# GpSimd's step additions on 64-bit words, and the products O x 1/sum on VectorE, in a fused gated mix of softmax and linear attention

## The chip, the cores and the metric

One core of a Trainium2 chip runs the whole program. The metric is the device time of one execution in microseconds (us), the median of several runs. The profile is one further execution, recorded by the hardware profiler. It tells of TensorE (PE, with its weight loads as PEld), VectorE (DVE), ScalarE (ACT), GpSimd (POOL) and the queue of SyncE (SP), which issues most DMAs.

## The reference

Two attention blocks read the same x (2048 rows, 512 columns, bf16) and are mixed row by row with a gate g. H is 32 heads of 16 columns.

```
x = A_x
g = sigmoid((x * gate_w).sum(-1, keepdims=True))
# A: softmax attention
q, k, v = heads of x @ A_wqkv
p = softmax(q k^T * Dh**-0.5)
a = (p v, heads joined) @ A_wo
# B: linear attention
phi(t) = where(t > 0, t + 1, exp(t)) + 1e-6
num = phi(q) (phi(k)^T v);  den = phi(q) sum(phi(k)) + 1e-6
b = (num / den, heads joined) @ B_wo
return g * a + (1 - g) * b
```

## The kernel before, in words

The work is one long sequence of score tiles. A *unit* is one tile of scores for one head: 128 keys by 512 queries. Heads go in groups of eight (t8, four groups), queries in four blocks of 512 (qc), and each group and block makes two rounds of four heads each (half), 32 rounds in all. A round has 64 units, the whole kernel 2048. PE multiplies three or four units side by side (f_mm, line 685, Qpad and KT into PSUM). Each unit's exponential is then made in one of two ways:

- ScalarE makes it exactly: one ACTIVATE (line 2071) takes two or three PSUM banks, 1024 or 1536 columns, and writes bf16 tiles PT. PE multiplies each with V once.
- VectorE takes a unit as a *claim*: one TENSOR_SCALAR (line 1565) evicts the scores to int16 in DP, so that the bits, read as f16, are a piecewise linear 2^x. One such pattern is not exact enough, so each claimed unit is used as three patterns (STEPS, line 31: the pattern itself and the pattern plus 342 and plus 683), each multiplied with V in its own scaling (WEIGHTS, line 30; the scaled copies of V are written at line 925). Four claimed units share one buffer of DP, of which there are 13 (line 236), and the two patterns with a constant added each fill a further buffer.

These additions, the *step additions*, take 128 x 2048 int16 values. Function try_close (line 1587) makes them. Either VectorE adds the constant to int16 (line 1606), or GpSimd does (line 1609): there a pair of int16 patterns is read as one int32 word, and a two-operand addition adds a word of the small tile `steps` that holds the constant twice. `steps` is written by two GpSimd memsets at the start (line 735).

At the end of a pair of rounds the accumulated numerator and the sum of the softmax lie in `oraw` (evicted by VectorE, line 1306). Small DMAs collect the sums, VectorE inverts them (line 1279), a DMA broadcasts 1/sum to `rbc`, and the product oraw x rbc goes to `OT` (line 1294). With OT_POOL = 1 the product is GpSimd's except in the last eight rounds, where it is VectorE's.

The order of all instructions is laid down when the program is built, by a planner that keeps a clock for each engine. It books each instruction with a duration (for instance POOL_ADD, line 447, for a step addition on GpSimd) and gives the next piece of work to whoever is free by its clocks: pool_go (line 494) hands an addition to GpSimd if it can start there soon, pump (line 571) gives VectorE what is left, can_claim (line 1521) decides whether VectorE takes another unit from ScalarE, depending among other things on free DP buffers. So a booked duration changes the order on every engine. An engine runs its instructions in the order laid down; where one needs another engine's result it waits on a semaphore. GpSimd's instructions also wait for the last VectorE instruction that had SBUF operands alone (line 530, _emit).

The start: the first rows of x and the first slices of the weights are loaded; GpSimd writes some constants (lines 702 to 764), among them a 128 x 128 identity `identb` (a memset, line 736, and an affine select, line 737) and the masks `maskK` and `maskQ`; PE transposes x with the identity (line 692), VectorE and ScalarE copy the transposes to xT (lines 1909 and 1907), PE multiplies xT with the weights, VectorE evicts the first queries with `maskQ` (line 887), and the first units follow. Between the memset and the affine select the program carries one instruction that names a library of GpSimd code, number 0. The profile has no row for such an instruction.

The last round has its own end: what has been accumulated is copied out once, the remaining products with V are accumulated in another layout (128x52 matmuls of Vaug with DP and PT), then normalised, transposed and multiplied with the output weights.

Of the kernel before, what the change touches and what calls it, by code (L numbers as in the profile page):

```python
# [9 lines left out]
ALU = mybir.AluOpType  # L10
# [2 lines left out]
BF16 = mybir.dt.bfloat16  # L13
I32 = mybir.dt.int32
I16 = mybir.dt.int16
U16 = mybir.dt.uint16

STATS = {}
# [11 lines left out]
WEIGHTS = (1.0, 203 / 256, 161 / 256)  # L30
STEPS = (0, 342, 683)
NG4 = len(STEPS)
Y_EXP = 12


# [177 lines left out]
def bass_gated_mix__mha_block__linear_attn_block__prompt_kernel(  # L213
# [33 lines left out]
    with ExitStack() as es:  # L247
        _cnt = [0]

        def SB(shape, dt, name):  # L250
            _cnt[0] += 1
            return es.enter_context(nc.sbuf_tensor(f"{name}_{_cnt[0]}", list(shape), dt))
# [27 lines left out]
        V20 = NG * VG  # L280
        Z0 = V20 + 2 * (NG4 - 1) * (V2C + PAD)
        Vraw = SB([128, Z0 + 32], BF16, "Vaug")
# [5 lines left out]
        def v_scaled(par, z, kb, n=1):  # L288

            c = V20 + ((NG4 - 1) * par + z - 1) * (V2C + PAD) + (kb - KB2) * 8 * VC  # L290
            return Vraw[:, c:c + n * 8 * VC]
# [11 lines left out]
        DP = SB([128, NB, NTU], BF16, "DP")  # L303
# [5 lines left out]
        rbc = SB([128, 512], FP32, "rbc")  # L309
        dev = SB([128, 2, 128], FP32, "dev")  # L310
        flag = SB([128, 1], I32, "flag")
        steps = SB([128, 4], I16, "step")
        epool = SB([128, 2, 512], BF16, "epool")
        KVbd = SB([128, NCC, 128], BF16, "KVbd")
        Zsel = SB([128, NCC, 8], BF16, "Zsel")
# [38 lines left out]
        PO = _Eng("pool", SEM("s_pool"))  # L354
# [19 lines left out]
        R = _Res  # L374
# [20 lines left out]
        r_OT = [[R(f"OT{t}_{q}") for q in range(NQC)] for t in range(NT8)]  # L395
        r_rraw = [R(f"rraw{k}") for k in range(8)]
        r_dev, r_flag = R("dev"), R("flag")
        r_step = R("step")
        r_e = [R("e0"), R("e1")]
        r_phiK = [[R(f"phiK{s}_{k}") for k in range(4)] for s in range(2)]  # L400
        r_phi2 = [R(f"phi2{k}") for k in range(NTB // 2)]
# [42 lines left out]
        YIELD_SOON = 0.5  # L444
        POOL_TT = 1.3
        POOL_V = 0.9
        POOL_ADD = 1.97
        OT_POOL = 1
        V2_POOL = 0

        def conflicts(op_, reads, writes):
# [96 lines left out]
        def op(E, fn, reads=(), writes=(), dur=0.2, issue=None):  # L548
            settle(reads, writes)
            return _emit(E, fn, reads, writes, dur, issue)  # L550
# [140 lines left out]
        def f_tr(o, i):  # L691
# [12 lines left out]
           dur=1.6)  # L704
# [9 lines left out]
        for t in range(1, NQC):  # L714
            for cc in range(NCD):
                dma(xT[:, cc, 512 * t:512 * (t + 1)], x2[512 * t:512 * (t + 1), 128 * cc:128 * (cc + 1)], semXT[cc][t],
                    writes=[r_xT[cc][t]], total_after=16, transpose=True, E=SP, lands=5.5)
# [13 lines left out]
                                                   pattern=pattern, channel_multiplier=mult), reads=[w], writes=[w])  # L731

        op(PO, lambda: nc.gpsimd.memset(warm[:], 0.0), writes=[r_warm])
        for z in range(1, NG4):
            op(PO, lambda z=z: nc.gpsimd.memset(steps[:, 2 * z - 2:2 * z], STEPS[z]), writes=[r_step], dur=0.1)  # L735
        op(PO, lambda: nc.gpsimd.memset(identb[:], 0.0), writes=[r_ident])
        op(PO, lambda: nc.gpsimd.affine_select(out=identb[:], in_=identb[:], compare_op=ALU.not_equal,
                                               fill=1.0, base=0, pattern=[[-1, 128]], channel_multiplier=1),
# [813 lines left out]
        def claim(r, u, b, beside, in_group=False):  # L1552
# [7 lines left out]
            if not in_group:  # L1560
# [3 lines left out]
                r_bank[b].tw = max(r_bank[b].tw, PE.t + 0.08)  # L1564
            push(0 if in_group else 1, [(lambda: nc.vector.tensor_scalar(DP[:, i, 512 * k:512 * (k + 1)].bitcast(I16),  # L1565
                                                                     bank_ap(b), FRAC - Y_BIAS4, Y_BIAS4, op0=ALU.max, op1=ALU.add),
# [5 lines left out]
        def add_products(i, z, k, r, u):  # L1572
            pv_pending.append((r, u, [(DP[:, i, 512 * k:512 * (k + 1)].bitcast(F16), z)], r_DP[i][k], Fraction(1, NG4)))

# [12 lines left out]
        def try_close():  # L1587

            while closing:
                i, us, zs = closing[0]  # L1590
                z = len(zs) + 1
                if z == NG4:
                    closing.popleft()
                    continue
                free = free_buffers()
                early = us[0][0] > acc_round[0]
                if len(free) < (LAZY if early else 1):
                    return False
                if not zs and sum(1 for it in items if it.prio == 3) >= (EARLY_ADDS if early else MOST_ADDS):
                    return False  # L1600
                i2 = free[0]
                zs.append(i2)
                n = 512 * len(us)
                y = DP[:, i, 0:n].bitcast(I16)
                mine_, out_ = r_DP[i][0:len(us)], r_DP[i2][0:len(us)]
                ops = (lambda z=z, i2=i2, y=y, n=n: nc.vector.tensor_single_scalar(DP[:, i2, 0:n].bitcast(I16), y, STEPS[z], ALU.add),  # L1606
                       mine_, out_, d_sb(n, 0.25), None)
                if n == NTU:
                    ops = (ops[0], mine_ + [r_step], out_, ops[3], None, POOL_ADD, lambda z=z, i2=i2, y=DP[:, i, 0:n].bitcast(I32), n=n: nc.gpsimd.tensor_tensor(  # L1609
                        DP[:, i2, 0:n].bitcast(I32), y, steps[:, 2 * z - 2:2 * z].bitcast(I32).to_broadcast([128, n // 2]), ALU.add))  # L1610
                push(3, [ops])
                of_round[iseq[0]] = us[0][0]
                for k, (r, u) in enumerate(us):
                    add_products(i2, z, k, r, u)
            return True
# [319 lines left out]
        for c in range(2):  # L1935
            for st, w, b, pcs in pair:
                fns, _, dur, mac, mode = pcs[c]
# [50 lines left out]
        while True:  # L1988
# [72 lines left out]
            for c, eb in extras:  # L2061
# [4 lines left out]
                     dur=QK_T, mac=0.053 * len(fns), mode="rows")  # L2066
            for c, eb in extras:
                claim(c[0], c[1], eb, True, in_group=True)
            STATS["claims %d+%d" % (len(us), len(extras))] = STATS.get("claims %d+%d" % (len(us), len(extras)), 0) + 1
            n = 512 * len(us)  # L2070
# [3 lines left out]
               dur=d_act(n), issue=0.055 + n * 8.34e-4)  # L2074
# [59 lines left out]
        while pv_pending:  # L2134
            if not pv_step(PE.t, force=True):
# [9 lines left out]
                 writes=[r_bank[tbank]], dur=0.3)  # L2145
# [8 lines left out]
           writes=[r_bad], dur=0.25)  # L2154
# [15 lines left out]
        for k in range(NPRE):  # L2170
# [6 lines left out]
            if k == 0:  # L2177
# [4 lines left out]
                         writes=[r_bank[tbank]], dur=0.1)  # L2182
# [47 lines left out]
        for t8 in range(NT8):  # L2230
# [11 lines left out]
            for qc in range(NQC):  # L2242
                for h in range(8):
# [4 lines left out]
                                                                      None, op0=ALU.mult),  # L2248
                       reads=[r_Q2, r_mask], writes=[r_Q[0]])
                    for k in range(4):  # L2250
# [4 lines left out]
                           writes=[r_sm] + r_rdB)  # L2255
# [16 lines left out]
        for tb in range(NTB):  # L2272
            s3 = tb % NOUTT
            pe_macro(out_fns(bank_ap(tb % 4), tb, order_out), reads=[r_OT[t][tb // 4] for t in range(NT8)] + [r_OBT[tb], r_woA, r_woB],
                     writes=[r_bank[tb % 4]])
# [87 lines left out]
```

## Time and profile before

| | us |
|---|---|
| median of 3 runs | 675.92 (675.24 to 676.07) |
| span of the profiled execution, first to last instruction | 673.6 |
| ScalarE busy | 660.1 (98%) |
| TensorE busy | 654.8 (97%) |
| VectorE busy | 575.6 (85%) |
| GpSimd busy | 550.6 (82%) |

The profiled execution has no time of its own beside its span; the median is 2.3 us above the span. The granted TensorE clock is 0.999 of full speed.

In rows of groups, the columns are: line of the kernel, engine, operation, output<-inputs with shapes and types, count | busy time in us, mean duration in ns | idle time of the engine just before these instructions and what ended most of it. A row of the waits says who waited for whom, the total in us, how often, and the longest. A row of the timeline or of the chain begins with the start in us and the length in us. A row for one line gives the shortest, median and longest duration in ns, and the first and last start. A DMA row gives the tiles, the count, KB each and the median time from issue to landing in us. ScalarE's instructions overlap, so that the mean duration is longer than the distance between two starts.

### The profile page before, as it was taken

The numbers are of one execution on the slowest core, as the hardware profiler recorded it, in microseconds if no ns is written. First come the engines' busy times: TensorE is split into PE (matmuls) and PEld (weight loads), VectorE is DVE, ScalarE is ACT, GpSimd is POOL, SyncE is SP. The second block draws the span as 40 slices with busy tenths as digits, with TensorE's granted clock in tenths as the row PEclk, the third lists the DMA queues.
The fourth block names the chain that finished last, engine by engine and source line by source line (L and its number), as shares of the span: only waits on it lengthen the run. The fifth ranks groups of instructions, "written<-read, shape, count | busy, mean of one in ns | idle before, by whom it ended". The sixth has DMA issues, their size and how long they took to land.

```text
span 673.6 us, 19206 instructions
## 1 busy us (share of the span) xinstructions
PE 654.8 (97%) x8078; PEld 199.8 (30%) x8078; DVE 575.6 (85%) x968; ACT 660.1 (98%) x715; POOL 550.6 (82%) x311
## 2 busy tenths in 40 slices
PE   8999999999999999999999999999999999999997
PEld 4322223333223332333222323323323222222223
DVE  4589889889887886888988998999889998989894
ACT  6999999999999999999999999999999999999995
POOL 5098889887889997788986989778788888898883
PEclk9999999999999999999999999999999999999999
DMA  9900101001010021101001010010211401010011
GB/s 212 261 3 12 24 2 33 3 11 27 1 35 2 18 50 36 32 2 30 6 10 36 9 40 12 16 29 13 47 25 25 51 25 42 10 41 27 20 40 44
DMA packets 44816, 22.96 MB, mean 34 GB/s; under 512 B 33976, under 2 KB 40568, under 8 KB 44728
## 3 DMA queue, kind: packets, MB, share of 16 engines
q1 hardware_dynamic: 42712, 20.12, 13.8%
q10 hardware_dynamic: 2016, 1.57, 0.9%
q8 instruction: 66, 1.08, 0.7%
q14 instruction: 22, 0.18, 0.1%
HBM read 8.00 MB, written 2.10 MB: 15 GB/s over the span
## 4 chain that ended last, share of the span: by engine, by line
ACT 89%; PE 7%; DVE 2%; DMA 1%; POOL 0%; issue 0%; SPq 0%; DVEq 0%; ACTq 0%
ACT PT L2071 87%; PE ps L685 7%; ACT epool L970 2%; DVE DP L1565 1%; DMA outt<-in_A_wqkv_dram 1%; POOL DP L1609 0%; DMA rsum<-oraw 0%; DVE DP L2173 0%; DVE KT L859 0%; DVE Qpad L887 0%; DVE OB L1098 0%; DVE oraw L1306 0%; SPq L608 0%; DVE rraw L1279 0%; PE ps L692 0%
## 5 line engine op out<-in xcount | busy, mean ns | idle before, releaser
L2071 ACT ACTIVATE PT<-ps 128x1024 bf16<-128x1024 f32 (+1 forms) x675 | 648.2, 1156 | 1.0 <-PE ps L685 0.7
L1609 POOL TENSOR_TENSOR DP<-DP,step 128x1024 int32<-128x1024 int32 x278 | 526.8, 1924 | 99.9 <-DVE DP L1565 27.6
L1565 DVE TENSOR_SCALAR DP<-ps 128x512 int16<-128x512 f32 x654 | 432.5, 684 | 69.5 <-PE ps L685 63.2
L685 PE MATMUL ps<-Qpad,KT 32*128 32x512 bf16 x2048 | 264.6, 384 | 10.4 <-ACT PT L2071 4.5
L685 PE MATMUL ps<-DP,Vaug 128*32 128x512 f16 x1949 | 206.8, 384 | 1.5 <-DVE oraw L1306 0.7
L685 PE MATMUL ps<-PT,Vaug 128*32 128x512 bf16 x1384 | 174.3, 384 | 0.6 <-DVE Vaug L914 0.5
L685 PEld LDWEIGHTS ps<-Qpad,KT 32*128 32x128 bf16 x2048 | 66.6, 91 | 270.3 <-ACT PT L2071 242.7
L685 PEld LDWEIGHTS ps<-DP,Vaug 128*32 128x32 bf16 x1949 | 49.7, 94 | 66.1 <-issue 41.3
L685 PEld LDWEIGHTS ps<-PT,Vaug 128*32 128x32 bf16 x1384 | 42.1, 95 | 46.7 <-issue 36.7
L685 PE MATMUL ps<-warm 128*32 128x512 bf16 (+1 forms) x270 | 45.8, 386 | 1.1 <-POOL step L735 1.1
L1606 DVE TENSOR_SCALAR DP<-DP 128x2048 int16<-128x2048 int16 (+1 forms) x50 | 33.1, 689 | 0.0
L685 PE MATMUL ps<-xT,wA 128*32 128x512 bf16 x432 | 32.6, 384 | 0.0
L1294 POOL TENSOR_TENSOR OT<-oraw,rbc 128x512 bf16<-128x512 f32 x12 | 15.6, 1299 | 10.9 <-DVE DP L1606 7.2
L970 ACT ACTIVATE epool<-ps 128x512 bf16<-128x512 f32 x32 | 23.4, 732 | 0.0
L1306 DVE COPY oraw<-ps 128x512 f32<-128x512 f32 x31 | 21.1, 681 | 0.7 <-PE ps L685 0.5
L685 PE MATMUL ps<-xT,wB 128*32 128x512 bf16 x256 | 19.7, 384 | 0.0
L685 PE MATMUL ps<-wB,xT 128*32 128x512 bf16 x256 | 19.3, 384 | 0.0
L685 PE MATMUL ps<-woA,OT 128*32 128x512 bf16 (+1 forms) x226 | 19.1, 384 | 0.0
L975 DVE SCALAR_TENSOR_TENSOR phi<-ps,epool 128x512 bf16<-128x512 f32 x24 | 16.3, 679 | 0.0
L685 PEld LDWEIGHTS ps<-warm 128*32 128x32 bf16 (+1 forms) x270 | 11.4, 98 | 13.6 <-issue 11.8
L859 DVE CAST KT<-ps 128x512 bf16<-128x512 f32 (+1 forms) x16 | 10.7, 666 | 5.2 <-PE ps L685 5.2
L685 PE MATMUL ps<-wA,xT 128*128 128x128 bf16 x192 | 14.9, 220 | 0.0
(106 smaller groups left out, 244.7 us busy)
## 6 DMA issues: line engine op xcount, KB each, us to landing
rbc<-oraw SPq DMA_DIRECT2D x16, 256.0 KB
OT<-in_A_x_dram SPq DMA_DIRECT2D x4, 512.0 KB, 6.9
Qpad<-Qs SPq DMA_DIRECT2D x124, 16.0 KB, 1.8
oraw<-oraw SPq DMA_DIRECT2D x60, 32.0 KB, 1.9
wA<-in_A_wqkv_dram SPq DMA_DIRECT2D x1, 1536.0 KB, 7.5
wB<-in_B_wqkv_dram SPq DMA_DIRECT2D x1, 1536.0 KB, 7.8
out_dram<-outt SPq DMA_DIRECT2D x12, 128.0 KB, 1.7
phi<-in_A_x_dram ACTq DMA_DIRECT2D x3, 256.0 KB, 6.0
```

Of the source, the lines that this page charges most:

```text
L685: return lambda: nc.tensor.matmul(o, lhsT=l, rhs=r, start=start, stop=stop, skip_group_check=sg)
L859: push(1, [(lambda: nc.vector.tensor_copy(KT[:, par, c0:c1], src), [r_bank[b]], [r_KT[par][t]], d_psum(n), None)])
L970: op(AC, lambda: nc.scalar.activation(epool[:, s, :], bank_ap(b), ACT.Exp), reads=[r_bank[b]], writes=[r_e[s]], dur=0.6, issue=0.48)
L975: (lambda: nc.vector.scalar_tensor_tensor(out=dst, in0=bank_ap(b), scalar=0.0, in1=epool[:, s, :], op0=ALU.max, op1=ALU.add), [r_bank[b], ...
L1294: push(1, [(lambda: (nc.gpsimd if on_pool else nc.vector).tensor_tensor(OT[:, t8, 512 * qc:512 * (qc + 1)], oraw[:, 0, :], rbc[:], ALU.mul ...
L1306: push(0, [(lambda: nc.vector.tensor_copy(oraw[:, half, :], acc), [r_acc], [r_oraw[half]], d_psum(512), evicted)])
L1565: push(0 if in_group else 1, [(lambda: nc.vector.tensor_scalar(DP[:, i, 512 * k:512 * (k + 1)].bitcast(I16), bank_ap(b), FRAC - Y_BIAS4, Y ...
L1606: ops = (lambda z=z, i2=i2, y=y, n=n: nc.vector.tensor_single_scalar(DP[:, i2, 0:n].bitcast(I16), y, STEPS[z], ALU.add), mine_, out_, d_sb ...
L1609: ops = (ops[0], mine_ + [r_step], out_, ops[3], None, POOL_ADD, lambda z=z, i2=i2, y=DP[:, i, 0:n].bitcast(I32), n=n: nc.gpsimd.tensor_te ...
L2071: op(AC, lambda p0=p0, b0=b0, n=n: nc.scalar.activation(PT[:, 512 * p0:512 * p0 + n], ps[:, 512 * b0:512 * b0 + n], ACT.Exp, scale=LN2 / F ...
```

## The change

Three things are changed in the source.

1. A step addition on GpSimd is no longer a two-operand addition over 128 x 1024 int32 words. It is one int64_add over 128 x 512 words of 64 bits, each holding four patterns, and the constant stands in the instruction, four times side by side (FOUR). The tile `steps` and its two memsets are gone, and with them what waited for `steps`.
2. POOL_ADD, the duration that the planner books for it, is 1.15 instead of 1.97.
3. OT_POOL is 0 instead of 1: all products oraw x rbc go to VectorE.

```diff
+I64 = mybir.dt.int64
...
+FOUR = 1 + (1 << 16) + (1 << 32) + (1 << 48)
...
-        steps = SB([128, 4], I16, "step")
...
-        r_step = R("step")
...
-        POOL_ADD = 1.97
-        OT_POOL = 1
+        POOL_ADD = 1.15
+        OT_POOL = 0
...
-        for z in range(1, NG4):
-            op(PO, lambda z=z: nc.gpsimd.memset(steps[:, 2 * z - 2:2 * z], STEPS[z]), writes=[r_step], dur=0.1)
...
                 if n == NTU:
-                    ops = (ops[0], mine_ + [r_step], out_, ops[3], None, POOL_ADD, lambda z=z, i2=i2, y=DP[:, i, 0:n].bitcast(I32), n=n: nc.gpsimd.tensor_tensor(
-                        DP[:, i2, 0:n].bitcast(I32), y, steps[:, 2 * z - 2:2 * z].bitcast(I32).to_broadcast([128, n // 2]), ALU.add))
+                    ops = (*ops[:4], None, POOL_ADD, lambda z=z, i2=i2, i=i, n=n: nc.gpsimd.int64_add(
+                        DP[:, i2, 0:n].bitcast(I64), DP[:, i, 0:n].bitcast(I64), STEPS[z] * FOUR))
```

Since the planner lays the order down anew, the instruction counts of the two programs differ (main path):

| | before | after |
|---|---|---|
| step additions on GpSimd | 278 | 320 |
| step additions on VectorE | 50 | 12 |
| products oraw x rbc on GpSimd / VectorE | 12 / 3 | 0 / 15 |
| units claimed by VectorE | 654 | 664 |
| ScalarE's exponentials of 1024 / 1536 / 512 columns | 629 / 45 / 1 | 626 / 44 / 0 |
| PE's products with V, 32x512 of DP / of PT | 1949 / 1384 | 1987 / 1373 |
| last round's 128x52 products, of DP / of PT | 52 / 40 | 20 / 44 |
| idle-time matmuls on `warm`, 32x512 / 128x512 | 188 / 80 | 148 / 70 |

int64_add stands in another library of GpSimd code than the affine selects. The changed program has the instruction that names library 0 ahead of the first affine select, as before, and one that names library 1, directly behind the last constant (Osb, line 762 of the changed kernel) and ahead of the first step addition and its wait. No later instruction names a library.

## The prediction

> **What bounds the kernel now.** I read the page's first part and its chain, then the groups with shapes kept apart, then the waits.
>
> ```profile
> span 673.6 us, 19206 instructions
> PE 654.8 (97%) x8078; PEld 199.8 (30%) x8078; DVE 575.6 (85%) x968; ACT 660.1 (98%) x715; POOL 550.6 (82%) x311
> ACT 89%; PE 7%; DVE 2%; DMA 1%; POOL 0%; issue 0%; SPq 0%; DVEq 0%; ACTq 0%
> ```
>
> ```profile
> L2071 ACT ACTIVATE PT<-ps 128x1024 bf16<-128x1024 f32 x629 | 591.1, 1131 | 0.1
> L1609 POOL TENSOR_TENSOR DP<-DP,step 128x1024 int32<-128x1024 int32 x278 | 526.8, 1924 | 99.9 <-DVE DP L1565 27.6 <-DVE epool L973 21.7 <-DVE DP L1606 15.4
> L1565 DVE TENSOR_SCALAR DP<-ps 128x512 int16<-128x512 f32 x654 | 432.5, 684 | 69.5 <-PE ps L685 63.2
> L2071 ACT ACTIVATE PT<-ps 128x1536 bf16<-128x1536 f32 x45 | 65.1, 1517 | 0.9 <-PE ps L685 0.7
> L2071 ACT ACTIVATE PT<-ps 128x512 bf16<-128x512 f32 x1 | 0.6, 602 | 0.0
> ```
>
> ```profile
> PEld ps L685 <- ACT PT L2071: 242.7, 567, 0.9
> PEld ps L685 <- POOL DP L1609: 10.1, 37, 0.5
> ```
>
> ScalarE is the bound: 675 exponentials with some 1.0 us of idle time ahead of all of them. PE's 97% is not a second bound: 567 times it waits, 0.43 us on average, for ScalarE to free a PSUM bank. It also waits 37 times for a GpSimd addition, 0.3 us on average, and ScalarE shows none of that: a GpSimd result that is late by less than about 0.43 us is absorbed. GpSimd is off the chain (0%). So the time falls only if ScalarE gets less to do, or starts or ends otherwise.
>
> **The change, part by part.**
>
> *ScalarE's share.* I counted both programs. The planner books an addition at 1.15 us where it booked 1.97, and so hands VectorE 664 of the 2048 score tiles (L1565) instead of 654. ScalarE's exponentials become 626 of 1024 and 44 of 1536, where it had 629, 45 and one of 512. The mean durations overlap (629 x 1.131 is 711 us, busy is 591.1), so I take the spacing in the chain:
>
> ```profile
> 10.59 4.14 ACT PT L2071 x3
> 55.55 11.00 ACT PT L2071 x12
> ```
>
> The first row is three of 1536 columns, 1.38 us each, the second gives 0.917 us for 1024. For the one of 512 I take 0.48, between 0.39 (0.602 less the overlap of 0.21 of the 1024 form) and 0.60. ScalarE saves 3 x 0.917 + 1.38 + 0.48 = **4.6 us**.
>
> *The tail.* Behind the last exponential PE has 40 matmuls of PT and then 16 of DP, whose addition ran late on VectorE:
>
> ```profile
> 666.23 0.56 PE L685 MATMUL ps<-Vaug,DP 128*128 128x52 bf16 x16
> 666.63 1.02 PE L685 MATMUL ps<-woB,OBT 128*128 128x512 bf16 x4
> ```
>
> The changed program ends with the 40 of PT, its 20 of DP being ahead of them: **0.4 us** less (666.63 - 666.23).
>
> *VectorE.* It gains ten evictions (10 x 0.66 = 6.6 us) and the 12 products, and loses 38 of its 50 own additions.
>
> ```profile
> L1606 DVE TENSOR_SCALAR DP<-DP 128x2048 int16<-128x2048 int16 (+1 forms) x50 | 33.1, 689 | 0.0
> L1294 POOL TENSOR_TENSOR OT<-oraw,rbc 128x512 bf16<-128x512 f32 x12 | 15.6, 1299 | 10.9 <-DVE DP L1606 7.2
> L1294 DVE TENSOR_TENSOR OT<-oraw,rbc x3: 680/681/681, 568.7 to 646.0; 128x512 bf16<-128x512 f32 x3
> ```
>
> That is +6.6 + 12 x 0.68 - 38 x 0.66 = -10 us, on an engine idle for 98 us of the span: nothing on the path. A product waits for the broadcast of 1/sum; on VectorE the evictions are queued behind it, and PE and ScalarE behind those. The three products already there cost no idle time, so 0; if the broadcast came late, at worst the queue stands for that lateness, and the 0.43 us of PE's slack goes first.
>
> *The new addition.* The trace has no 64-bit addition. From above it is bounded by the two-operand addition, 1.892 us; from below by one pass over 1024 words at the rate of the memset, 5.004 / 5888 = 0.85 ns an element, 0.87 us.
>
> ```profile
> 3.88 5.00 POOL L760 MEMSET Vaug<- 128x5888 bf16 x1 [0.45 <-DVE maskQ L758]
> L1609 POOL TENSOR_TENSOR DP<-DP,step x278: 1885/1892/2396, 32.4 to 660.7; 128x1024 int32<-128x1024 int32 x139
> ```
>
> The booked 1.97 is 0.08 above the median of 1.892, so the 1.15 now booked stands for about 1.07 us. One operand fewer is read, so I take the end near the memset, 1.07. The order is fixed by the bookings, so a still faster addition gains nothing; up to 1.07 + 0.43 = 1.5 us PE's slack covers a slower one. Sum: 0.
>
> *Two changes of GpSimd's code.* The changed program has one instruction, ahead of the first affine select, that names code library 0 (as before's has) and a new one, ahead of the first addition, that names library 1. Nothing names 0 again at the end. So an execution that follows another one starts with library 1 in place and has to bring back 0. In before only 0 is ever named:
>
> ```profile
> 0.97 0.26 POOL L735 MEMSET step<- 128x2 int16 x2
> 1.16 0.21 POOL L736 MEMSET identb<- 128x128 bf16 x1
> 1.60 0.29 POOL L737 TENSOR_SCALAR_AFFINE_SELECT identb<-identb 128x128 bf16<-128x128 bf16 x1 [0.23 <-POOL identb L736]
> 4.61 1.07 PE L692 MATMUL ps<-identb,PT 128*128 128x128 bf16 x16
> 5.95 0.62 PE L685 MATMUL ps<-xT,outt 128*32 128x512 bf16 x8 [0.28 <-DVE xT L1909]
> 6.88 1.05 PE L685 MATMUL ps<-xT,outt 128*32 128x256 bf16 x24 [0.32 <-DMA outt<-in_A_wqkv_dram]
> 9.76 0.53 POOL L764 MEMSET Osb<- 128x512 bf16 x1
> 32.44 5.59 POOL L1609 TENSOR_TENSOR DP<-DP,step 128x1024 int32<-128x1024 int32 x3 [22.15 <-DVE DP L1565]
> ```
>
> Where the library is already there, naming it costs at most the 0.23 us. Where it isn't, code must come by DMA while the first loads fill the queues. The nearest rows are loads of this kernel:
>
> ```profile
> phi<-in_A_x_dram ACTq DMA_DIRECT2D x3, 256.0 KB, 6.0
> wB<-in_B_wqkv_dram SPq DMA_DIRECT2D x1, 1536.0 KB, 7.8
> out_dram<-outt SPq DMA_DIRECT2D x12, 128.0 KB, 1.7
> ```
>
> Bounds 0 and 7.8 us; I take 6.0, the loads issued in the same microsecond. GpSimd reaches this point 0.19 us earlier (1.16 - 0.97, two memsets having gone). Without the gap the affine select would end at 1.60 - 0.19 - 0.23 + 0.29 = 1.5; with 6.0 for the exchange and 0.1 for signalling the identity is there at 7.6 us, and the transposes that need it start then instead of at 4.61. They had 0.31 us to spare (5.95 + 0.62 = 6.57 against the weights at 6.88). The start moves by 7.6 - 4.61 - 0.31 = **2.7 us**, and with ScalarE never idle afterwards so does the end. The masks come right behind and are needed later. Library 1 is loaded in the gap from 10.29 to 32.44: shifted by 6 us, 16 us are left and hide it; without that cover the first three additions would be late by its length.
>
> The Trainium skill (GPSIMD Engine Reference, § 2.1 Instruction dispatch) has a rule that speaks against this change: the first call into a freshly loaded library pays about 6 us (5.95) with no instruction of its own in the profile. By that figure the shift would be 2.6 us, an estimate, and the time 673.5; the 0.23 us of before doesn't contradict it, since nothing is exchanged there.
>
> **The sum.** 673.6 - 4.6 - 0.4 + 2.7 = 671.3 us of span. The median of the runs, 675.92, is 2.3 above before's span, which I keep as constant: **673.6 us**, 0.34% less.
>
> **The rivals.**
>
> *No exchange at the start* (0.22). Library 0 is in place at each start, or comes at no visible cost: the 0.23 us speaks for it, that nothing names 0 at the end against. Then 675.92 - 5.0 = 670.9.
>
> *A long exchange* (0.22). Removing and loading are two steps, amid the loads. Beyond 7.7 us (shift 7.7 - 3.3 = 4.4) it takes nearly the whole gain, beyond 9.7 it makes the kernel slower by over 0.2%. From 7.5 to 11: 675.1 to 678.6. The DMA's share of 0.9 in the first slice of the page speaks for it:
>
> ```profile
> DMA  9900101001010021101001010010211401010011
> ```
>
> *Additions longer than their place* (0.18), which makes the kernel slower. Two halves with a carry may take GpSimd as long as two operands did. It decides from about 1.5 us, where PE's slack ends. At 1.892 GpSimd itself becomes the bound: start 35 us, 320 x 1.85 = 592 (three take 5.59, so they start (5.59 - 1.89) / 2 = 1.85 apart), waits for VectorE 99.9 - 22.1 = 78, tail 673.6 - 660.7 = 13: 718 us. Just beyond 1.5 some 0.1 us times 320 is not absorbed, with some of it overlapping: 680 to 700. Against it: one operand is read, not two.
>
> That the change doesn't do what it says is no rival here: all 320 additions and 15 products stand where it puts them.
>
> **How the numbers follow.** The forecast's own case (0.38) goes with an exchange of 4 to 7.5 us: 671.6 to 675.1. The measurement tells apart about 0.2%, 1.35 us: faster is below 674.6, slower above 677.3. Faster: 0.22, and 0.34 of the forecast's 0.38: 0.56. Slower: the additions 0.18 and 0.09 of the long exchange, 0.27. The same: the rest, 0.17. The range 670.3 to 681 leaves out most of the long additions and little else.
>
> **What would show it.** Right: 320 additions of 1.0 to 1.2 us; the first transposes near 7.6 us behind a gap of some 6 us ahead of the first affine select; the first exponential about 2.7 us later than now; ScalarE without idle time from there on, PE still waiting for it hundreds of times; the last DP matmuls ahead of the last PT ones. Wrong: transposes at 4.6 (no exchange), or beyond 9.5 (a long one); PE's waits for additions beyond some 50 us with ScalarE idle behind PE; an eviction stalled behind a product.

## The result, and the profile after

| | before | after |
|---|---|---|
| median (lowest to highest), 5 runs each | 675.85 (675.24 to 676.07) | 678.61 (677.98 to 679.15) |
| span of the profiled execution | 673.6 | 677.0 |

The ratio is 1.0044 (95% interval 1.0032 to 1.0057): the changed kernel is slower by 0.44%. I had forecast 673.6, faster.

First the page of the changed kernel: the span, the busy times, the granted clock in 40 slices and the chain's shares.

```profile
span 677.0 us, 19101 instructions
...
PE 649.5 (96%) x8028; PEld 199.0 (29%) x8028; DVE 565.1 (83%) x952; ACT 655.0 (97%) x710; POOL 343.0 (51%) x339
...
PEclk7999999999999999999999999999999999999999
...
ACT 93%; PE 4%; issue 2%; DVE 1%; POOL 0%; POOLq 0%; ACTq 0%
```

ScalarE is busy 5.1 us less (660.1 before) and is still the bound, yet the span is 3.4 us longer. Two entries stand out: "issue" has 2% of the chain (0% before), and the first slice of the clock is 7 tenths (9 before).

Next the groups of the changed kernel (the product's row with shapes kept apart):

```profile
L2069 ACT ACTIVATE PT<-ps 128x1024 bf16<-128x1024 f32 (+1 forms) x670 | 643.1, 1160 | 1.0 <-PE ps L685 0.9
L1563 DVE TENSOR_SCALAR DP<-ps 128x512 int16<-128x512 f32 x664 | 439.4, 686 | 72.4 <-PE ps L685 66.3
L1607 POOL INT64_ADD DP<-DP x320 | 334.6, 1055 | 307.3 <-DVE DP L1563 223.7
L1292 DVE TENSOR_TENSOR OT<-oraw,rbc 128x512 bf16<-128x512 f32 x15 | 10.2, 682 | 0.0
```

The 670 exponentials still have 1.0 us of idle time ahead of them in all, and the 15 products none. The body of the kernel is as forecast. The loss lies ahead of the first exponential, as its timeline shows (start, length, engine, line; in brackets the idle time before and what ended it):

```profile
0.96 0.20 POOL L734 MEMSET identb<- 128x128 bf16 x1
12.28 0.28 POOL L735 TENSOR_SCALAR_AFFINE_SELECT identb<-identb 128x128 bf16<-128x128 bf16 x1 [11.12 <-issue]
19.91 0.53 POOL L762 MEMSET Osb<- 128x512 bf16 x1
...
1.08 3.77 PE L685 MATMUL ps<-warm 128*128 128x512 bf16 x9 [1.08 <-POOL warm L733]
12.71 1.86 PE L692 MATMUL ps<-identb,PT 128*128 128x128 bf16 x16 [7.85 <-POOL maskK L738]
14.50 2.75 PE L685 MATMUL ps<-xT,outt 128*32 128x512 bf16 x32
...
18.59 12.53 ACT L2069 ACTIVATE PT<-ps 128x1536 bf16<-128x1536 f32 x9 [0.91 <-PE ps L685]
...
644.22 25.13 ACT L2069 ACTIVATE PT<-ps 128x1024 bf16<-128x1024 f32 x24
```

GpSimd stands still for 11.1 us ahead of the first affine select, and the timeline names nothing that it waits for. The view of that source line does have rows for the naming of the library, contrary to what I wrote above of the profile:

```profile
L735 POOLq MODIFY_POOL_CONFIG  x2: 11/11/11, 1.4 to 1.4; - x2
```

The two instructions run at 1.4 us and take 11 ns each; the affine select starts 10.9 us later. All that needs the identity stands with it: the transposes begin at 12.71 instead of 4.61. They are also slower, 1.86 us for the same sixteen that took 1.07. The last row of the timeline gives the end of the exponentials, 644.22 + 25.13 = 669.35. The same two ends in the timeline of the kernel before:

```profile
9.11 21.15 ACT L2071 ACTIVATE PT<-ps 128x1536 bf16<-128x1536 f32 x17 [0.74 <-PE ps L685]
...
644.39 20.73 ACT L2071 ACTIVATE PT<-ps 128x1024 bf16<-128x1024 f32 x20
```

So the span splits into three:

| | before | after | difference | forecast |
|---|---|---|---|---|
| start to first exponential | 9.11 | 18.59 | +9.5 | +2.7 |
| first to last exponential | 656.0 | 650.8 | -5.2 | -4.6 |
| behind the last exponential | 8.4 | 7.6 | -0.8 | -0.4 |

The windows of the changed kernel tell why PE is slow behind the gap. The columns are the window, its length, busy time and count for PE, PEld, DVE, ACT and POOL, then the granted clock, the DMA share and GB/s.

```profile
4.00:8.00 4.00, 0.85 (x3) 0.15 (x1) 0.00 (x0) 0.00 (x0) 0.00 (x0) 0.99 1.26 278
8.00:12.00 4.00, 0.00 (x0) 0.00 (x0) 0.00 (x0) 0.00 (x0) 0.00 (x0) 0.50 1.08 182
14.00:16.00 2.00, 2.00 (x26) 1.06 (x27) 0.71 (x2) 0.92 (x2) 2.00 (x2) 0.50 0.97 362
18.00:20.00 2.00, 1.79 (x28) 0.81 (x28) 0.98 (x3) 1.42 (x1) 1.94 (x5) 0.97 0.11 13
```

PE ran out of its nine idle-time matmuls at 4.85 us. From about 7.9 us on the granted clock is 0.50, and it stays there until some 18 us, through the transposes and the first projections.

### The profile page after: what moved, and what is told of

Its sections match the earlier page's. It is cut to its first block, busy times and chain, and to the rows that moved or that the text cites. A ratio compares the mean times of both kernels' runs of the same rounds, so it can differ in the third digit from the quotient of the medians.

```text
span 677.0 us, 19101 instructions
## 1 busy us (share of the span) xinstructions
PE 649.5 (96%) x8028; PEld 199.0 (29%) x8028; DVE 565.1 (83%) x952; ACT 655.0 (97%) x710; POOL 343.0 (51%) x339
## 2 busy tenths in 40 slices
DMA packets 44816, 22.96 MB, mean 34 GB/s; under 512 B 33976, under 2 KB 40568, under 8 KB 44728
## 3 DMA queue, kind: packets, MB, share of 16 engines
q8 instruction: 66, 1.08, 0.7%
## 4 chain that ended last, share of the span: by engine, by line
ACT 93%; PE 4%; issue 2%; DVE 1%; POOL 0%; POOLq 0%; ACTq 0%
ACT PT L2069 90%; PE ps L685 4%; ACT epool L968 2%; PE ps L692 0%; DVE DP L2171 0%; DVE epool L1402 0%; DVE epool L1403 0%; DVE KT L857 0%; POOL identb L735 0%; DVE DP L2176 0%; DVE flag L2181 0%; POOL identb L734 0%; POOL warm L733 0%; POOL dummy L702 0%; ACT eg L952 0%
## 5 line engine op out<-in xcount | busy, mean ns | idle before, releaser
L1563 DVE TENSOR_SCALAR DP<-ps 128x512 int16<-128x512 f32 x664 | 439.4, 686 | 72.4 <-PE ps L685 66.3
L1607 POOL INT64_ADD DP<-DP x320 | 334.6, 1055 | 307.3 <-DVE DP L1563 223.7
L685 PE MATMUL ps<-DP,Vaug 128*32 128x512 f16 x1987 | 203.7, 384 | 1.7 <-DVE oraw L1304 1.5
L685 PE MATMUL ps<-PT,Vaug 128*32 128x512 bf16 x1373 | 169.9, 384 | 0.5 <-DVE Vaug L912 0.5
L685 PEld LDWEIGHTS ps<-PT,Vaug 128*32 128x32 bf16 x1373 | 40.6, 95 | 46.9 <-issue 36.0
L685 PE MATMUL ps<-warm 128*32 128x512 bf16 (+2 forms) x221 | 39.9, 391 | 1.1 <-POOL warm L733 1.1
L912 DVE CAST Vaug<-ps 128x512 bf16<-128x512 f32 x16 | 10.9, 684 | 3.6 <-PE ps L685 3.6
L685 PEld LDWEIGHTS ps<-wA,xT 128*128 128x128 bf16 x192 | 10.8, 98 | 5.4 <-issue 5.0
```

The lines of the kernel that those rows point to most:

```text
L685: return lambda: nc.tensor.matmul(o, lhsT=l, rhs=r, start=start, stop=stop, skip_group_check=sg)
L912: ops = [(lambda: nc.vector.tensor_copy(v_group(NQC * par + v)[:, :, :, 0:16], src), [r_bank[b]], [r_V[par][v]], d_psum(512), lambda: v_do ...
L1607: ops = (*ops[:4], None, POOL_ADD, lambda z=z, i2=i2, i=i, n=n: nc.gpsimd.int64_add(DP[:, i2, 0:n].bitcast(I64), DP[:, i, 0:n].bitcast(I64 ...
```

## The experiments

All kernels below compute the whole result. Times are medians on the same chip as a run of the kernel before, which was at 675.5 to 675.7 each time. The first four ask what the gap at the start is, the next five what the rest of the change is worth by its parts, and the last four how long an exchange of libraries takes, and where.

**One library for the whole program.** An affine select can run from library 1 too, as this run shows, so the changed kernel can do without library 0.

```diff
         op(PO, lambda: nc.gpsimd.memset(warm[:], 0.0), writes=[r_warm])
+        PO.ops.append(([], lambda: nc.gpsimd.load_library(library_config.all_libraries[1]), False, None))
         op(PO, lambda: nc.gpsimd.memset(identb[:], 0.0), writes=[r_ident])
```

> The changed kernel, but it names library 1 once, ahead of the identity, and runs the affine selects from it too; it never names library 0. Theory (what costs is the exchange of one library for another; naming the one that is in place costs nothing): an execution that follows another finds library 1 in place, the affine select starts at about 1.5 us as in before, transposes at 4.6, first exponential at 9.1. The changed kernel's start was 9.5 us late (18.59 against 9.11), its exponentials took 5.3 us less (650.8 against 656.0) and its tail 0.8 less (7.6 against 8.4), so the time is 675.9 - 6.1 = 669.8. Rival (naming library 1, or running from it, costs a load in every execution): 11 us ahead of the first affine select again, time 678.6.

Measured: 669.51 (669.31 to 669.58), ratio 0.9908 (0.9895 to 0.9922). The page's span and the row of its timeline for the first affine select:

```profile
span 667.8 us, 19099 instructions
```

```profile
1.50 0.29 POOL L736 TENSOR_SCALAR_AFFINE_SELECT identb<-identb 128x128 bf16<-128x128 bf16 x1 [0.16 <-POOL identb L735]
```

The gap of 11.1 us is 0.16 us, and the kernel is 9.1 us faster than the changed one with the same order of work. The gap is the naming of a library that isn't in place. That naming one that is in place costs next to nothing holds as before.

**Library 0 named again at the end,** behind the last addition, so that the next execution finds it.

```diff
+        PO.ops.append(([], lambda: nc.gpsimd.load_library(library_config.all_libraries[0]), False, None))
```

> The changed kernel with one more instruction behind GpSimd's last addition, which names library 0 again. Theory (the start pays because the execution before left library 1 in place): no gap at the start, first exponential at 9.1 us; the exchange back begins at about 653 us, where the last addition ends, and lies beside the tail, which ends near 667; with 7 to 11 us it ends by 664 and is hidden: 669.8, up to 672 if it takes longer than the tail. Rival (a program that names two libraries loads each of them whenever it is named): the start keeps its 11 us, and the time is 678.6 or more.

Measured: 669.37 (669.10 to 670.01), ratio 0.991 (0.9897 to 0.9924). Its timeline has the first affine select at once again:

```profile
1.66 0.29 POOL L735 TENSOR_SCALAR_AFFINE_SELECT identb<-identb 128x128 bf16<-128x128 bf16 x1 [0.49 <-POOL identb L734]
```

Nothing at the start of this program differs from the changed kernel. What differs is what the execution before left behind. So the library outlives the execution.

**The kernel before, leaving library 1 behind.** The converse: the kernel before, with all its instructions, names library 1 behind its last addition.

```diff
+        PO.ops.append(([], lambda: nc.gpsimd.load_library(library_config.all_libraries[1]), False, None))
```

> The kernel before, with one more instruction behind GpSimd's last addition that names library 1; no 64-bit addition, the same order. Theory: each execution finds library 1 in place, the affine select waits 11 us, PE's clock falls, and the first exponential comes 9.5 us later than in before: 675.9 + 9.5 = 685.4, 684 to 687. Rival (the delay belongs to the new additions or to the new order): 675.9.

Measured: 684.74 (684.19 to 684.83), ratio 1.0133 (1.0117 to 1.0148), 9.1 us more. Its timeline shows the same start as the changed kernel's, without any 64-bit addition:

```profile
12.19 0.28 POOL L737 TENSOR_SCALAR_AFFINE_SELECT identb<-identb 128x128 bf16<-128x128 bf16 x1 [10.83 <-issue]
...
12.61 1.86 PE L692 MATMUL ps<-identb,PT 128*128 128x128 bf16 x16 [7.55 <-POOL maskK L740]
```

The three runs together settle where the 9.1 us come from.

**PE kept busy through the gap,** the changed kernel with 44 idle-time matmuls instead of 9.

```diff
-        warm_up(9, 0)
+        warm_up(44, 0)
```

> The changed kernel with 44 instead of 9 matmuls on the tile warm at the start, so that PE works until about 12 us. The exchange alone would move the first transposes by 8.1 us (12.71 against 4.61), less the 0.3 they had to spare: 7.8; the first exponential moved by 9.5. Theory (the other 1.7 us are the granted clock, 0.5 from 8 to 18 us because PE stood idle): the clock stays at 1.0, the first exponential comes at about 16.9 instead of 18.6, the time is 678.6 - 1.7 = 676.9. Rival (the 1.7 us come from something else, such as DMAs delayed by the exchange): 678.6.

Measured: 677.02 (676.66 to 677.58, 11 runs), ratio 1.0023 (1.0014 to 1.0032), 1.6 us less than the changed kernel. PE in its timeline:

```profile
1.08 11.70 PE L685 MATMUL ps<-warm 128*128 128x512 bf16 x44 [1.08 <-POOL warm L733]
12.79 1.05 PE L692 MATMUL ps<-identb,PT 128*128 128x128 bf16 x16
14.12 1.48 PE L685 MATMUL ps<-xT,outt 128*32 128x512 bf16 x32 [0.28 <-DVE xT L1907]
```

The exchange is as long as ever, but the transposes take 1.05 us and the projections 1.48 where they took 1.86 and 2.75. The first exponential comes at 16.77 instead of 18.59, and the granted clock is 1.00 in all windows from 4 to 20 us. So 1.6 of the 9.1 us, by the medians, was PE's clock.

**The old booking,** on top of the kernel with one library: the same additions, booked at 1.97.

```diff
-        POOL_ADD = 1.15
+        POOL_ADD = 1.97
```

> The one-library version with the 64-bit additions booked at 1.97 us as before: the new addition and the moved products without the new order. VectorE then claims 640 units, ScalarE has 606 exponentials of 1024, 65 of 1536 and one of 512. Theory (a shorter addition gives nothing by itself; only its booking, which hands units to VectorE, does): against before ScalarE has -23 x 0.917 + 20 x 1.36 = +6.1 us, so 675.6 + 6.1 = 681.7, and the same within 0.5 us as the next kernel, which has the same order and the long additions. Rival (a shorter addition frees PE of waits and shortens the time): several us below the next kernel.

Measured: 680.89 (680.49 to 681.05), ratio 1.0077 (1.006 to 1.0094).

**The products alone,** the kernel before with its own additions and booking.

```diff
-        OT_POOL = 1
+        OT_POOL = 0
```

> The kernel before with only the products moved to VectorE: int32 additions, booked at 1.97. Its order is that of the kernel above: 640 units claimed, 606, 65 and 1 exponentials. Theory (the products' 12 places on VectorE are paid by claims that it no longer takes): 681.7. Rival, as the prediction had it (nothing on the path, the products lie in VectorE's idle time): 675.6.

Measured: 681.28 (680.82 to 681.55), ratio 1.0084 (1.0067 to 1.0101). Its groups, shapes apart:

```profile
L1565 DVE TENSOR_SCALAR DP<-ps 128x512 int16<-128x512 f32 x640 | 423.0, 686 | 74.0 <-PE ps L685 67.2
L1294 DVE TENSOR_TENSOR OT<-oraw,rbc 128x512 bf16<-128x512 f32 x15 | 10.3, 688 | 2.5 <-DMA rbc<-oraw 2.5
```

The products stall for 2.5 us in all, and yet their move costs 5.6 us: the planner now gives VectorE 640 units where it gave 654, so ScalarE gets 14 more. The two runs together: with the products moved, the addition that takes 1.04 us instead of 1.89 gives 0.4 us, which the two ranges don't tell from nothing, as long as the planner books it as before. The booking gives 680.89 - 669.51 = 11.4 us. The whole change in parts is then 675.85 + 5.6 (products) - 0.4 (addition) - 11.4 (booking) + 9.1 (start) = 678.75, against 678.61. That the two meet confirms nothing: the kernels form a chain from before to after, each a step from the last, so the steps have to add up. The parts belong to this order of steps; another order, such as the booking without the moved products, wasn't run.

**Additions that are late for their place:** the changed kernel's order with the additions of the kernel before. It is made from the kernel before, with the changed kernel's booking and products, and has the changed kernel's counts (320 additions on GpSimd, 664 units claimed, 626 and 44 exponentials).

```diff
-        POOL_ADD = 1.97
-        OT_POOL = 1
+        POOL_ADD = 1.15
+        OT_POOL = 0
```

> The changed kernel's order (additions booked at 1.15 us, products on VectorE), but with the int32 additions of 1.892 us; one library alone, so no exchange. The prediction's rival of additions longer than their place: GpSimd becomes the bound, its 320 additions need 592 us and, with 78 us of waits, the time is 718. Where the waits disappear because GpSimd is always behind: 32 + 592 + 13 = 637 is below ScalarE's 669, so that the time lies between, 680 to 718, with ScalarE idle behind PE. Rival (PE's slack absorbs it): 670.

Measured: 732.19 (731.08 to 734.76), ratio 1.0833 (1.0815 to 1.0851), above both ends of what I expected. Its waits (who waited for whom, us in total, times, longest):

```profile
PEld ps L685 <- POOL DP L1609: 76.8, 110, 2.3
...
ACT PT L2071 <- PE ps L685: 48.1, 82, 2.6
```

The mechanism is the one named: PE waits for GpSimd, and ScalarE for PE. My price of 718 was low in two terms. The additions are busy for 602.8 us, where I had 592, and their waits come to 107.6 - 22.1 = 85.5 us, where I had copied 78 over from before.

**The products given back to GpSimd,** in the changed kernel. A product runs from library 0 and a 64-bit addition from library 1.

```diff
-        OT_POOL = 0
+        OT_POOL = 1
```

> The changed kernel with the 12 products back on GpSimd. The product's instruction belongs to library 0, the 64-bit addition to library 1, so that the program has two exchanges around each of the 12 products, 24 beside those at the start. Theory (an exchange of 7 to 11 us wherever the library isn't in place): GpSimd stands for 14 to 22 us at each product, far more than PE's slack, additions come late, and PE and ScalarE wait for part of it: about 678 + 12 x 12 = 820, 740 to 900. Rival (exchanges amid the kernel lie in GpSimd's 307 us of idle time): below 690.

Measured: 798.51 (one run). Its waits:

```profile
ACT PT L2069 <- PE ps L685: 114.9, 55, 12.1
...
POOL OT L1292 <- issue: 86.2, 12, 7.6
...
POOL DP L1607 <- issue: 58.2, 10, 6.0
```

Twelve times 7.2 us to library 0 (6.7 to 7.6), and 5.8 us each for ten of the ways back, and ScalarE waits for PE for 114.9 us, where the changed kernel's exponentials were idle for 1.0. So the third part of the change isn't free to choose: with the new addition, each product left on GpSimd costs two exchanges.

**Two other bookings,** 1.20 and 1.25, on top of the kernel with one library.

```diff
-        POOL_ADD = 1.15
+        POOL_ADD = 1.20
```

> The one-library version with the addition booked at 1.20 us instead of 1.15. The order comes out another time: ScalarE has 637 exponentials of 1024, 38 of 1536 and one of 512. By the spacings 0.917, 1.36 and 0.48 that is +11 x 0.917 - 6 x 1.36 + 0.48 = +2.4 us against the one-library version at 1.15 (669.5). Theory (the time follows ScalarE's exponentials as the planner deals them out, and a small change of a booking shifts them by some us either way): 671.9. Rival (the booking has to be right, and the time has a minimum at the measured 1.04 + 0.08 = 1.12, with little change close by): 669.5 within 1.

> The same with 1.25 us: 633 exponentials of 1024, 36 of 1536 and one of 512: +7 x 0.917 - 8 x 1.36 + 0.48 = -4.0 us against 669.5. Theory: 665.5, the fastest of all. Rival: the farther the booking is from 1.12, the slower, above 671.9.

Measured: 677.56 (677.26 to 678.93), ratio 1.0034 (1.0021 to 1.0046), for 1.20, and **666.67** (666.54 to 667.09), ratio 0.987 (0.9853 to 0.9886), for 1.25, which beats both kernels. ScalarE's 1024- and 1536-column exponentials are 637 and 38 for 1.20, 633 and 36 for 1.25, 626 and 44 for 1.15; the two new orders have one of 512 as well. By my spacings that is 2.3 us more than 1.15, and 4.1 less. The chain's shares, first of 1.20, then of 1.25:

```profile
ACT 71%; PE 25%; DVE 2%; DMA 2%; issue 0%; POOL 0%; SPq 0%; DVEq 0%; ACTq 0%; POOLq 0%
```

```profile
ACT 84%; PE 12%; DVE 1%; DMA 1%; issue 0%; SPq 0%; POOL 0%; ACTq 0%; POOLq 0%
```

At 1.25 the counts explain the gain (4.1 by the counts; the body is 647.8 against 651.1 at 1.15, the time 2.8 less). At 1.20 the kernel loses 8 us, more than either expectation had, and the counts explain only 2.3 of it: the body is 656.9, the end behind it 9.4 instead of 7.6, the start half a microsecond later. PE has a quarter of that chain, which suggests that in this order ScalarE is no longer the only bound. That is read from the chain alone; no run shows it, and which pieces of PE's work would do it stays open.

**Why 10.9 us at the start, when it is about 7 in the middle?** My first reading was the loads: the DMA share is 1.26 and 1.08 in the windows above. To the kernel with one library I added one pair of exchanges, with a small addition between them that only library 0 has, first behind the last constant (10.3 us), and in another kernel ahead of the 30th step addition (87 us). `probe` is a tile of four columns, and each kernel zeroes it at its start.

```diff
+            nc.gpsimd.load_library(library_config.all_libraries[0])
+            nc.gpsimd.tensor_tensor(probe[:, 2:4], probe[:, 0:2], probe[:, 0:2], ALU.add)
+            nc.gpsimd.load_library(library_config.all_libraries[1])
```

> The kernel that starts with library 1, with one exchange to library 0, a four-column product-like addition that needs it, and one exchange back to library 1, directly behind the last constant (Osb, end at 10.3 us). The loads still run there: the DMA share is 0.87 to 1.03 from 10 to 18 us. It is the first use of library 0 in this execution. Theory (the exchange at the start takes 10.9 us because its code queues behind the loads): the small addition starts 9 to 11 us behind Osb, at 19.5 to 21.5 us. Rival 1 (it depends on the start of the program, not on the loads): 7.2 us behind, as in the middle of the kernel with the products given back. Rival 2 (the first use of a library in an execution is the long one, whatever the loads do): 10.9 us here too, and 10.9 in the twin that has the pair at about 90 us. Under each the second exchange ends ahead of the first step addition at 32.4 us, so the time is that of the kernel that starts with library 1: 669.5, within 0.7.

> The same pair of exchanges, also the first use of library 0 in the execution, ahead of the 30th step addition, at about 85 to 90 us, where the DMA share is 0.01. Theory (loads in the way): 7.2 us to library 0 and 5.8 back to library 1, as in the middle of the kernel with the products given back. Rival 2 (first use is long): 10.9 to library 0. The time: 13 us of GpSimd with additions queued behind it; a pair there cost (798.5 - 678.6) / 12 = 10.0 us of the end, so 669.5 + 10.0 = 679.5 by that, and from 672 up if the planner's 13 buffers and the idle half of GpSimd make up for some of it.

Measured: 669.04 and 683.68 (one run each). The timeline of the first, then of the second:

```profile
17.52 0.18 POOL L768 TENSOR_TENSOR probe<-probe 128x2 f32<-128x2 f32 x1 [7.25 <-issue]
```

```profile
95.59 0.18 POOL L768 TENSOR_TENSOR probe<-probe 128x2 f32<-128x2 f32 x1 [8.17 <-issue]
101.75 3.06 POOL L776 INT64_ADD DP<-DP  x3 [5.97 <-issue]
102.83 0.11 PEld L686 LDWEIGHTS ps<-DP,Vaug 128*32 128x32 bf16 x3 [12.62 <-POOL DP L776]
...
104.04 1.02 ACT L2083 ACTIVATE PT<-ps 128x1024 bf16<-128x1024 f32 x1 [12.64 <-PE ps L686]
```

The 8.17 us of the second run aren't all exchange. Its rows for the naming stand at 88.5 us, and the same addition of the kernel with one library, without a pair, also waited there, 1.08 us for VectorE:

```profile
L767 POOLq MODIFY_POOL_CONFIG  x2: 11/11/11, 88.5 to 88.5; - x2
```

```profile
88.52 2.05 POOL L1608 INT64_ADD DP<-DP  x2 [1.08 <-DVE DP L1564]
```

So that exchange took 95.59 - 88.5 = 7.1 us. My reading was wrong as it stood. At 10.3 us the DMA share is 0.59 to 1.03, and the exchange takes 7.25 us; at 88.5 us the share is 0.03 or less, and it takes 7.1. It isn't the first use of library 0 either, since both are that. The second run also shows that hardly anything buffers an exchange in the middle. The addition behind the pair starts 13.2 us late (101.75 against 88.52), ScalarE then stands for 12.64 us, and the time grows by 683.68 - 669.51 = 14.2 us. PE's clock fits the rest: PE stands still from 90.7 us, and the granted clock is 0.50 from 93.5 to 107. I had expected 672 to 679.5.

So two more, the pair behind the last mask (3.3 us) and behind the identity's memset (1.3 us).

> The kernel that starts with library 1, with the pair of exchanges (library 0, a small addition that needs it, library 1) behind the last mask, at about 3.3 us. Three theories for the 10.9 us at the start against 7.25 at 10.3 us: (a) the loads are fetched from 1 to 10 us at a DMA share of up to 1.3 and the code stands behind them; begun at 3.3 us it takes about as long as at 1.2, 9 to 11 us, so the small addition runs at 12.3 to 14.2; (b) something of the program's start has to be over first, at a fixed time: whatever asks for a library before then is served at 12.2 us, so it runs at about 12.2 and the exchange takes 8.9; (c) only the very first moments are special: 7.25, at 10.6. The time is 669.5 plus what the constants behind it, 13 to 17 us later than they were, cost the first products with V: up to 4 us, 669.5 to 674.

> The same pair behind the memset of the identity, at about 1.3 us, which is the exchange of the changed kernel's start with one more exchange back. All three theories have library 0 in place 10.9 us later, at about 12.2; another length would show that it isn't the place but what the execution before left that counts. Back to library 1 takes 5.8 to 6.0 us if loads don't matter, as at 90 us, and up to 10 if they do (a), so that the affine select of the identity runs at about 18.2, or at up to 22. The first exponential then comes some 6 us later than in the changed kernel, at 24.6, and the time is 678.6 - 9.1 + 6 + 9.4 = 684.9, less up to 1 us.

Measured: 676.36 and 687.32 (one run each). Timelines of the one at 3.3 us and of the one at 1.3 us:

```profile
13.17 0.18 POOL L750 TENSOR_TENSOR probe<-probe 128x2 f32<-128x2 f32 x1 [9.81 <-issue]
```

```profile
1.12 4.02 PE L686 MATMUL ps<-warm 128*128 128x512 bf16 x9 [1.12 <-POOL warm L736]
12.15 0.19 POOL L740 TENSOR_TENSOR probe<-probe 128x2 f32<-128x2 f32 x1 [10.78 <-issue]
20.94 0.28 POOL L742 TENSOR_SCALAR_AFFINE_SELECT identb<-identb 128x128 bf16<-128x128 bf16 x1 [8.60 <-issue]
21.37 1.86 PE L693 MATMUL ps<-identb,PT 128*128 128x128 bf16 x16 [16.22 <-POOL maskK L745]
```

The way back of the first of them shows in the next constant:

```profile
23.29 5.00 POOL L766 MEMSET Vaug<- 128x5888 bf16 x1 [9.93 <-DVE Vaug L920]
```

The row puts the wait down to VectorE, but the cast that it names had ended at 22.42 us, and the mask that this memset waits for in the program (maskQ) was there at 3.8. What it waited for was library 1, named at 13.6 us. From the naming to the next instruction on GpSimd:

| to library 0, named at | 1.3 to 1.6 us | 3.3 us | 10.2 us | 88.5 us | amid the kernel (12 times) |
|---|---|---|---|---|---|
| us | 10.6 to 11.0 | 9.8 | 7.3 | 7.1 | 6.7 to 7.6 |

| to library 1, named at | 12.6 us | 13.6 us | 96 us | amid the kernel (12 times) |
|---|---|---|---|---|
| us | 8.4 | 9.7 | 5.8 | 5.4 to 5.8 |

The first moments alone (c) are ruled out by 9.8. A fixed time at which all are served (b) missed as well: it said 12.2, and it was 13.17. Of the three, (a), the loads of the first ten microseconds, is the one whose numbers held at 3.3 us, and the two ways back amid the loads took 8.4 and 9.7 us where it took 5.8 at 96 us. But 7.3 amid the loads at 10.2 speaks against the DMA share as such. So all long exchanges were named in the first 14 us, and not all named there were long. What does it (which loads, which queue) stays open: the trace counts the same 44816 DMA packets and 22.96 MB for the kernel before, without an exchange, and for the one with the products given back, so it doesn't hold the exchange's own transfer. That it is neither library 0 nor its first use in the execution is shown. Each of these four kernels ran once. The time at 1.3 us was 2.4 above the 684.9 expected, for the way back took 8.4 and not 5.8 to 6.0; at 3.3 us it was 2.4 above the upper end, as the constants came 19 us late and ScalarE then stood for 5.25 us.

## Why the prediction was wrong, point by point

**The step that failed** is "two changes of GpSimd's code". It named the mechanism, the place and what would wait (an execution that follows another has to bring back library 0; identity, transposes, first exponential). It mis-sized one thing and put another at nothing.

- *The exchange.* "Bounds 0 and 7.8 us; I take 6.0", from the landing times of loads. The gap is 11.1 us, above the bound. Landing times of ordinary loads don't bound an exchange of code: it took 7.1 us with next to no load running (DMA share 0.03). With transposes at 12.71 instead of the forecast 7.6, this is 5.1 of the 6.8 us by which the start was missed. The Trainium skill (GPSIMD Engine Reference, § 2.1 Instruction dispatch) gives 5.95 us for it: only the way back in quiet places (5.4 to 5.8) is that short here; to library 0 it was 6.7 to 11.0, and the measurement decides.
- *PE's clock.* The forecast had the start move rigidly. From the transposes to the first exponential it took 5.88 us (18.59 - 12.71) instead of 4.50 - 0.31 = 4.19: 1.7 us more, which the kernel with 44 idle-time matmuls confirms. I asked what the late identity delays, but not what an idle PE does meanwhile. The Trainium skill (TensorE: Matmul & The Clock Gate, Part 1) has the rule that I missed: about 3.4 us of idle time put TensorE at half rate. The trace is near it, somewhat shorter: idle from 4.85 us, at 0.50 from about 7.9, so after 3.0 us.

**The rival** that came true is the long exchange, chance 0.22, priced at up to 678.6 for 11 us. That it met 678.61 is luck in part: it lacked the 1.7 us of the clock, while body and tail gained 1.1 us more than forecast and the median lies 1.6 us above this span instead of 2.3. That 2.3 was no constant of the kernels: executions whose time and span are both on record lie 1.8 apart (678.79 and 677.0 here, 675.75 and 674.0 for the kernel before), so the execution profiled before was most likely a little faster than its median.

**No exchange at the start** (0.22, 670.9) was wrong for the changed kernel, but the two kernels that take the exchange away show what its case was worth: 669.4 to 669.5.

**ScalarE's share** was right: -4.6 forecast, -5.2 measured, from the counts and the spacing in the chain.

**The tail** was right in its direction, -0.4 against -0.8. The order at the end is the one foreseen, DP's 20 ahead of PT's 40:

```profile
668.00 0.66 PE L685 MATMUL ps<-Vaug,DP 128*128 128x52 bf16 x20 [0.22 <-DVE epool L1403]
...
669.05 1.17 PE L685 MATMUL ps<-Vaug,PT 128*128 128x52 bf16 x40
```

**VectorE and the products.** No stall, as said; the row of 15 products has 0.0 us of idle time. "The products cost 0" is true of their waits alone. Their move takes 14 units from VectorE, worth 5.6 us, and I had that only inside the net count of ten units more. So the sum was right, and the reader of it would have taken the move for free.

**The new addition** was right: 1.07 us taken, 1.04 measured, with PE's slack covering what is late. One row of the line of the additions (duration shortest, median, longest in ns), then the waits of the changed kernel:

```profile
L1607 POOL INT64_ADD DP<-DP x320: 1032/1037/1527, 41.9 to 661.3; - x160
```

```profile
PEld ps L685 <- ACT PT L2069: 245.5, 572, 1.2
...
PEld ps L685 <- POOL DP L1607: 8.4, 32, 0.9
```

PE waits 32 times for GpSimd, 8.4 us in all, less than before (10.1), and ScalarE sees none of it. The rival of additions that are too long fell with that.

**Library 1** is exchanged in the gap behind Osb, as said: with the shift of 10 us the gap runs from 20.4 to the first addition at 41.9, which waits for VectorE. The naming is the first thing in it:

```profile
L1607 POOLq MODIFY_POOL_CONFIG  x2: 16/16/16, 20.6 to 20.7; - x2
```

## What to carry to other kernels

A library of GpSimd code stays in place from one execution to the next, so a program that ends in another library than it begins with pays an exchange at every start: use one library throughout, or name the first one again where GpSimd is idle at the end. Before a step near the start is allowed to become late, ask what an idle PE will run like afterwards. And where a planner lays the order down, the booked duration is a change of its own: here it was worth 11.4 us, the faster instruction under the old booking 0.4, and bookings 0.05 and 0.10 longer lost 8.0 and gained 2.8 us. The shorter booking pays only because the instruction is that fast: with the old additions in the new order the time was 732 us.

## What the runs showed of the hardware that wasn't expected

- What one execution leaves in GpSimd decides the start of the next: the kernel before became 9.1 us slower by one instruction behind its last addition.
- The exchange isn't one figure: 10.6 to 11.0 us to library 0 at the start, 6.7 to 7.6 from 10 us on; 5.4 to 5.8 to library 1 in quiet places, 8.4 and 9.7 at 12.6 and 13.6 us.
- PE at half speed shows in durations even where the granted clock doesn't: with the pair at 1.3 us PE had been idle for 16.2 us and the transposes took 1.86 us, as in the changed kernel, though the page of that run has 9 in all slices of the clock.
